# The same 2997 steps of a DeltaNet and MLP kernel, emitted in another stated order

## The chip, the cores and the metric

The kernel runs on one NeuronCore of a Trainium2 chip, in fp32. The metric is the device time of one execution in microseconds, median over the runs. Profiles come from one further execution under the hardware profiler; their "span" runs from the first to the last instruction.

## The reference, cut to what matters

Attention works on batch 4, 8 heads, 768 tokens and head dimension 48; the bridge puts the heads side by side into 384 columns, and a layernorm with an MLP 384 to 1536 to 384 follows.

```python
def _attn_ref(q, k, v, beta):
    k_n = k / (np.linalg.norm(k, axis=-1, keepdims=True) + 1e-06)
    state = np.zeros((B, H, D, D), dtype=np.float32)
    for t in range(S):
        kt, vt, bt = (k_n[:, :, t], v[:, :, t], beta[:, :, t, None])
        y[:, :, t] = np.einsum('bhd,bhde->bhe', q[:, :, t], state)
        v_old = np.einsum('bhde,bhd->bhe', state, kt)
        state = state + bt[:, :, :, None] * np.einsum('bhd,bhe->bhde', kt, vt - v_old)
    return y

def _moe_ref(x, g_ln, w_ch1, w_ch2):
    mu = np.mean(x, axis=-1, keepdims=True)
    var = np.mean((x - mu) ** 2, axis=-1, keepdims=True)
    xn = (x - mu) / np.sqrt(var + 1e-06) * g_ln
    ch = np.maximum(xn @ w_ch1, 0.0) @ w_ch2
    return x + ch
```

## The kernel before

The 768 tokens are cut into 12 chunks of 64. Inside a chunk the recurrence over tokens is turned into matrix products and the inverse of a triangular 64x64 matrix for each of the 32 batch-heads; between chunks a 48x48 state for each batch-head is carried on.

**Attention on TensorE.** All 32 batch-heads of a chunk are worked on together. One step of this kind issues 64 small matmuls, one for each of 32 heads in two passes of fp32, in tiles of 64*64 of the array, so that several heads run beside each other. `gram` and `queries` (L775) make the products k k' and q k'; `recur` makes the state's share of values and outputs (L983), the solved values u (L1017; L1000 for chunk 0), the output (L1024) and the state's update (L1034). Steps of 32*32 tiles, `join` (L898 and L904), put the halves of an inverse together.

**The inverse.** Chunk 0's is made by `first_inverse` on three engines, since all else waits for it: VectorE scales the products (L695), masks (L704) and transposes them (L710), then five rounds follow, each with two products E (L722) and two products Z (L741) on TensorE, one for each half of the heads, masked copies on VectorE (L731), transposes (L687) and copies on ScalarE (L681). The other chunks' 32x32 halves are inverted row by row on VectorE by `rows_inverse`, a multiply (L860) and a subtraction (L867) for each row, for two chunks at a time.

**MLP.** A chunk of 64 tokens of 4 batches is 256 rows. The first layer is L1326 and L1341 for chunk 0, L1300 for chunks 1 to 3, and `fifteen` (L1221), a product scheme with 15 products where the plain one has more, from chunk 4 on. The second layer is `seven` (L1423), a scheme of seven products on halves, with its sums and differences on POOL (L1410). These matmuls use the array as a whole (128*128). Ahead of them the layernorm (its reciprocal root on VectorE is L967) is made.

**Weights.** They come as 64-bit words in ten pieces (`fetch`, on ScalarE's DMA queue) and are turned into fp32 by `convert` on ScalarE (L524, L532), VectorE (L529) and POOL (L542).

**What sets the order.** The program first records steps: `add` notes a function that issues some instructions of one engine, and works out which earlier steps it depends on. `emit` then runs the steps in the sequence that the string `ORDER` states, each number one step and `a:b` a stretch; "z" is one additional full-array product whose result is used by nobody (L1515). A step may stand anywhere behind the steps that it depends on.

```python
    def emit(self):
        out = set()
        for n in stated_order():
            if n < 0:
                self.filler()
                continue
            fn, deps = self.steps[n]
            assert deps <= out and n not in out
            fn()
            out.add(n)
```

`in_this_order` ties every instruction to the one before it on its engine, and the DMA issues of SyncE and ScalarE to each other, so that the stated sequence is the sequence that runs. Only the order within each engine's own list (and of the DMA issues) has an effect on the chip.

Steps that the prediction names: 95 and 96 are the first products of chunk 0 (L635), 97 and 98 transposes for chunk 1 (L568); 110 and 116 are the scaling L695 for the two halves of the heads, 111 and 117 the masks L704, 112 and 118 the transposes L710; 122 and 124 are E1, 126 and 132 Z1, 144 and 150 Z2, 162 and 168 Z3, 180 and 186 Z4; 149 is a copy on ScalarE behind Z2, 161 a masked copy on VectorE ahead of Z3; 355 and 357 are L1000, 359 and 360 L1024 of chunk 0; 588 is the first product of the MLP (L1326). 51 loads a part of chunk 0's keys on SyncE's queue.

Of the kernel before, what the change touches and what calls it, by code (L numbers as in the profile page):

```python
# [59 lines left out]
1 9 49 50 8 63 52 51 10 5 250 54 71 11 56 0 6 14 7 12 47 62 53 48 23 13 72 55 36 18 64 42 26 37 61 27 58 60 77 81 15 28 17 32 331 43 73 88 29 40 65 79  # L60
24 19 82 68 78 21 89 74 95 16 76 20 90 75 98 83 80 84 22 85 34 91 86 96 87 33 25 92 97 93 4 35 30 94 110 99 100 111 101 112 114 66 116 122 113 211 210
117 102 70 208 123 115 103 118 233 126 104 124 69 127 105 107 128 119 31 121 106 125 120 252 129 223 132 38 221 138 108 134 39 139 109 222 251 140 135
204 131 130 234 136 3 674 144 137 67 57 133 213 254 146 224 141 149 2 209 413 235 44 142 147 45 253 244 212 143 256 145 150 255 242 205 41 154 153 416
155 243 148 238 151 236 332 152 225 675 156 z 215 157 240 159 158 214 237 239 160 216 162 161 257 46 241 168 164 166 333 206 165 334 245 207 417 163
419 169 174 170 343 258 226 175 172 259 173 415 171 176 381 177 425 260 227 261 167 178 344 217 228 180 179 248 414 263 345 335 386 346 219 182 262
677 186 264 181 420 183 265 266 192 267 268 189 246 336 269 270 218 193 229 220 188 185 184 187 59 271 196 422 190 272 191 231 273 426 194 274 197 199
275 198 421 338 276 247 355 382 277 195 249 384 356 337 359 278 678 279 679 280 200 230 281 361 232 363 387 339 282 364 201 383 391 283 202 203 385
389 373 357 284 375 388 376 374 396 285 590 390 340 358 341 588 591 286 681 342 401 379 287 392 288 289 594 394 290 953 291 347 589 595 292 348 380
293 360 393 350 598 294 362 395 592 368 599 349 442 295 680 441 406 296 351 427 369 815 593 444 297 814 428 443 298 676 602 424 299 352 687 596 300
603 353 301 445 302 399 303 304 377 597 612 305 817 306 606 354 307 418 308 613 607 309 365 423 600 310 397 311 614 689 312 601 366 313 610 314 816  # L70
315 615 611 316 409 604 317 819 318 319 616 818 605 320 404 321 617 322:324 407 608 398 483 325 378 400 402 326 367 629 487 609 370 481 403 371 618
630 480 429 372 446 627 486 485 619 682 628 405 482 633 484 631 329 634 408 330 447 632 410 327 328 448 449 956 479 821 635 820 411 637 809 620 810
638 488 636 621 489:491 641 492 494 622 639 430 493 691 623 495 640 690 496 642 431 497 686 498 624 499 500 822 643 435 434 693 645 501 433 962 502
688 432 503 644 651 957 1100 504 505 436 692 506 507 652 438 508 439 509 647 440 510 437 811 653 511 512 964 450 666 1102 513 654 514 1099 451 515 655
516 517 454 518 965 519 966 1104 520 656 961 455 521 951 456 452 522 463 958 457 646 458 657 453 1215 464 649 465 807 523 459 658 808 524 466 460 1105
525 659 963 467 461 1106 694 950 468 683 462 955 526 660 1112 527 684 1101 528 469 1111 529 473 648 650 695 530 475 474 531 470 476 532 471 661 472
696 533 857 534 1114 535 697 536 967 855 537 858 1213 538 539 685 662 540 856 541 823 542:545 825 546:548 861 663 549:551 863 552 862 553:556 667 867
557 864 968 668 665 869 824 879 868 702 880 959 664 960 859 1214 669 873 860 560 1272 559 672 1103 865 561 812 670 558 705 826 477 866 699 874 698 870
701 888 969 412 706 871 703 885 700 875 704 671 872 1216 566 881 889 625 876 877 895 563 1217 813 567 878 1222 890 564 569 915 882 570 827 562 891 568
886 898 571 565 916 707 1107 896 626 899 572 1115 1212 900 708 883 576 892 709 574 884 901 573 1224 710 1116 893 575 902 954 887 894 917 903 1380 1113  # L80
828 904 1221 1558 711 713 905 829 923 918 577 712 897 924 832 714 715 673 925 716 833 717 906 718 834 926 719 912 835 907 841 836 927 1274 842 919 928
837 1560 908 838 929 920 843 913 839 909 844 941 840 720 910 721 830 845 921 914 846 847 722 922 1377 851 723 578 1264 1223 849 930 724 1557 1226 579
942 725 580 1562 831 931 1218 852 943 850 1118 853 932 848 726 581 1117 933 854 727 582 944 911 728 934 945 729 935 730 970 936 1227 731 938 1376 583
732 937 971 1225 972 585 1273 1228 584 587 1210 1563 733 946 734 1006 952 735 939 736 737 1004 738 974 973 947 1005 739 1007 586 1028 1010 740 1029
1119 1564 1559 975 1229 1011 1031 1008 1561 741 1385 742 1570 940 743 1569 1012 744 1009 745 746 1016 747 1013 976 748 749 1014 1387 750 1017 1572
1386 751 478 1211 979 752 1571 1015 1378 753 754 977 980 755 981 756 1018 1389 757 988 982 989 1384 1573 978 990 1379 1020 983 758:760 1022 761 1021
762 991 984 763 1390 1019 764 1108 985 765 949 1023 1034 1391 766 1230 986 767 948 1109 768 769 1388 1037 770 987 771 1110 1026 772 773 992 774 775
993 994 1038 776 1027 1024 995 1670 1044 1231 996 1030 1120 1265 1025 1275 1047 1035 1121 1039 1064 1040 1048 1122 1045 780 1041 1032 777 1049 1033
778 1065 1042 1036 779 1050 1043 1066 1126 1046 1051 1000 1054 1219 1266 1233 998 1268 997 1232 1276 999 1267 1127 1052 1055 1131 1053 1067 1565 1128
1061 1056 1072 1124 1270 1068 1125 1073 1392 1220 1069 1129 1074 1002 1057 1130 1001 1070 1075 785 1003 784 1058 1269 1076 781 1234 1079 1277 782 1059  # L90
1080 1271 783 1060 1077 1081 1680 2035 1078 786 1373 1062 1090 787 1123 1082 790 1091 789 1083 788 1063 1278 1092 2037 1279 1084 1682 1132 1071 1093
1681 1085 791 1302 1133 1086 1280 793 1134 792 1135 794 1136 1138 795 1094 1284 1137 2039 1139 1140 1235 1141 1285 1142 1281 1143 796 1305 1095 1303
1236 1668 1290 2034 1096 1684 1144 1087 1374 1145 2041 1282 1146 1291 1673 2036 1147 1148 1574 1088 1149 1237 1150 1283 1669 1151 1152 1239 1098 1153
1154 797 1155 1156 1296 1157 799 800 1158 1241 1686 1159 1288 1576 1160 1297 1304 1248 1161 2040 1311 1162 1289 1286 1238 1249 1250 1163 1381 1294
1164 1858 1287 1382 1165 1240 1383 1679 801 1312 1675 1295 1292 1251 1089 1166 1167 1685 1313 1168 1293 1674 1393 1252 1242 1169 798 1253 1855 1308
1243 1395 1375 1309 1244 1857 1306 1245 802 1318 1397 1097 1314 1300 1394 1319 1307 1298 1170 1575 1301 1171 803 805 1172 1246 1321 1173 1315 1247
1174 1322 1299 1255 1316 804 1310 806 1323 1254 1317 1396 1175 1256 1320 1683 1176 2038 1398 1672 1177 1178 1324 1179 1399 1338 1180 1325 1676 1181
1339 1326 1340 1327 1328 1182 1341 1260 1346 1183 1342 1184 1257 1347 1185 1343 1186 1259 1348 1344 1329 1687 1258 1349 1335 1353 1330 1350 1187 1354
1863 1188 1331 1189 1853 1351 1190 1402 1336 1191 1263 1345 1352 1261 1400 1262 1192 1404 1193 1194 1355 1865 1411 1195 1332 1412 1196 1356 1197 1413
1364 1198 1333 1414 1365 1334 1337 1450 1199 1441 1366 1200 1401 1440 1451 1455 1201 1427 1403 2150 1577 1357 1405 1430 1406 1367 1851 1358 1457 1439  # L100
1566 1852 1415 1431 1456 1359 1416 1429 1407 1688 1443 1408 1859 1567 1432 1409 1418 1368 1444 1202 1452 1410 1435 1203 1369 1433 1204 1454 1458 1370
1205 2047 1453 1417 1208 1460 1434 1459 1419 1361 1862 1464 1442 1461 1568 1436 1462 1866 1466 1437 1671 1467 1463 1867 1438 1578 1465 1360 1445 1690
1362 1446 1469 1468 1579 1447 1689 1422 1428 1471 1448 1470 1449 1474 2049 1472 1477 1581 1584 1475 1473 1580 1480 1860 1423 1861 1478 1363 1483 1479
1481 1583 1476 1691 1421 1484 2051 1489 1420 1694 1486 1485 1582 1693 1490 1692 1487 1502 1496 1588 1491 1503 1587 1488 1677 1492 1678 1504 1695 1585
1493 1206 1505 1494 1586 1506 1497 1495 1371 1701 1426 1516 1869 1589 1498 1696 1703 1868 1507 1499 1699 1529 1207 1424 2042 1509 1697 1517 1372 1744
# [1547 lines left out]
```

## Time and profile before

| | |
|---|---|
| median of 3 runs | 507.94 us (506.93 to 510.24) |
| span of the profiled execution | 508.8 us, mean granted TensorE clock 0.965 |
| TensorE busy, by stretch: 0 to 15 / 15 to 44 / 44 to 66 us | 10.7 of 15 / 21.7 of 29 / 20.4 of 22 us |
| TensorE busy, 66 to 500 us | 431.2 of 434 us |
| TensorE's granted clock, 15 to 44 / 44 to 66 us | 0.59 / 0.77, else 1.00 until 500 us |
| VectorE, ScalarE, POOL busy from 66 to 500 us | 298, 203 and 239 of 434 us |
| start of the first MLP product (step 588) | 55.9 us |
| start of E1 (step 122) | 13.46 us |

The profiled execution has no run time of its own beside its span; the span is 0.9 us above the median of the runs and lies inside their spread. Busy time of a matmul record is from its start to a modelled end, so that consecutive records overlap; the distance from one start to the next is the better measure of what a step takes. Every fp32 matmul of the program appears as two records, a transpose as one.

### The profile page before, as it was taken

The page shows a single profiled execution, that of the slowest core. Times are in us where ns is not written, and L with a number is a line of the kernel's source. Part 1 is how long each engine was busy: PE and PEld are TensorE (multiplying, and loading weights), DVE is VectorE, ACT ScalarE, POOL GpSimd, SP SyncE. Part 2 cuts the span into 40 slices and gives each one's busy share as a digit, 9 for nine tenths or more (in the row PEclk, how much of TensorE's full clock was granted, in tenths as well). Part 3 has the DMA queues.
Part 4 walks back from the last instruction along what each step waited for, and adds up shares of the span by engine and source line. Part 5 has one row for each costly group of instructions (what it writes and reads, how often), then busy time and mean ns, then how long its engine had stood idle before and what let it go on. Part 6 is the DMA issues. An engine that isn't in the chain of part 4 may idle for free.

```text
span 508.8 us, 22190 instructions
## 1 busy us (share of the span) xinstructions
PE 488.6 (96%) x9606; PEld 447.6 (88%) x9606; DVE 353.8 (70%) x780; ACT 249.0 (49%) x620; POOL 275.6 (54%) x430
## 2 busy tenths in 40 slices
PE   7778999999899999999999999999999999999996
PEld 3667988788788898899999999999999999999996
DVE  9668987997679648896649898568899328143251
ACT  5758873643544524627435535435563257363230
POOL 5464537264755496438894363492543850645633
PEclk9756799999999999999999999999999999999999
DMA  8988796667656566546834434766154402211101
GB/s 168 293 160 190 249 200 85 98 152 130 90 86 87 187 119 119 65 99 149 194 58 62 94 62 135 150 94 97 50 92 106 111 20 45 60 48 46 24 18 31
DMA packets 196097, 54.99 MB, mean 108 GB/s; under 512 B 186076, under 2 KB 189404, under 8 KB 196000
## 3 DMA queue, kind: packets, MB, share of 16 engines
q1 hardware_dynamic: 189920, 40.58, 41.9%
q10 hardware_dynamic: 3872, 9.83, 6.0%
q0 software_dynamic: 2208, 3.17, 3.8%
q8 instruction: 75, 1.23, 1.0%
q14 instruction: 22, 0.18, 0.1%
HBM read 36.64 MB, written 16.91 MB: 105 GB/s over the span
## 4 chain that ended last, share of the span: by engine, by line
PE 90%; DVE 5%; issue 2%; POOL 1%; DMA 1%; SPq 0%; ACT 0%; DVEq 0%; POOLq 0%; ACTq 0%
PE f L1423 29%; PE f L1221 22%; PE f L1300 9%; PE f L1326 4%; PE f L1341 3%; PE by L983 2%; PE by L1024 2%; PE two L983 2%; PE by L775 2%; PE two L1017 2%; PE two L775 2%; PE two L1034 2%; PE f L775 1%; DMA xt<-xd 1%; PE by L741 1%
## 5 line engine op out<-in xcount | busy, mean ns | idle before, releaser
L1410 POOL TENSOR_TENSOR h_all<-h_all 128x256 f32<-128x256 f32 x123 | 89.9, 742 | 135.1 <-PE f L1423 121.3
L1423 PE MATMUL f<-w_sb,h_all 128*128 128x192 f32 x492 | 109.8, 332 | 1.6 <-DVE rstd L967 1.6
L1423 PEld LDWEIGHTS f<-w_sb,h_all 128*128 128x128 f32 x492 | 81.8, 190 | 3.6 <-issue 1.9
L1423 PE MATMUL f<-words,h_all 128*128 128x192 f32 x396 | 84.5, 330 | 0.3 <-POOL h_all L1410 0.3
L860 DVE TENSOR_TENSOR tmp<-xb,gb 128x87 f32<-128x87 f32 (+21 forms) x186 | 73.7, 396 | 4.9
L867 DVE TENSOR_TENSOR xb<-xb,tmp 128x87 f32<-128x87 f32 (+21 forms) x186 | 73.6, 396 | 4.8
L1241 DVE TENSOR_TENSOR h_all<-h_all,f 128x512 f32<-128x512 f32 x96 | 63.5, 682 | 14.3 <-PE f L1221 13.2
L1423 PEld LDWEIGHTS f<-words,h_all 128*128 128x128 f32 x396 | 66.6, 190 | 1.7 <-POOL h_all L1410 1.0
L1300 PE MATMUL f<-xnt,w_sb 128*128 128x256 f32 x216 | 50.2, 382 | 0.0
L349 POOL DMA_DIRECT2D tb<-in_k_dram x64 | 42.0, 660 | 10.3 <-DVE kt L755 9.4
L1243 ACT ACTIVATE h_all<-h_all 128x512 f32<-128x512 f32 x48 | 28.5, 624 | 34.6 <-DVE h_all L1241 34.3
L1300 PEld LDWEIGHTS f<-xnt,w_sb 128*128 128x128 f32 x216 | 40.2, 190 | 5.3
L1237 ACT COPY h_all<-f 128x512 f32<-128x512 f32 x48 | 26.2, 590 | 34.3 <-PE f L1221 17.4
L1441 DVE TENSOR_TENSOR o<-f,x 128x192 f32<-128x192 f32 x33 | 11.6, 352 | 38.9 <-PE f L1423 22.3
L1221 PE MATMUL f<-words,w_sb 128*128 128x128 f32 x256 | 31.7, 276 | 0.0
L1309 ACT ACTIVATE h_all<-f 128x256 f32<-128x256 f32 x36 | 13.3, 382 | 35.1 <-PE f L1300 34.9
L1221 PEld LDWEIGHTS f<-words,w_sb 128*128 128x128 f32 x256 | 30.0, 192 | 0.2
L1221 PE MATMUL f<-xnt,w_sb 128*128 128x128 f32 x192 | 25.4, 276 | 0.0
L542 POOL TENSOR_TENSOR w_sb<-words 128x768 uint32<-128x768 uint32 (+1 forms) x11 | 15.0, 1365 | 17.7 <-DVE words L529 13.3
L1221 PEld LDWEIGHTS f<-xnt,w_sb 128*128 128x128 f32 x192 | 23.7, 192 | 0.1
L1326 PEld LDWEIGHTS f<-xnt,w_sb 128*128 128x128 f32 x144 | 19.2, 200 | 3.3 <-issue 0.2
L1088 ACT ACTIVATE xnt<-xnt,g_sb 128x256 f32<-128x256 f32 x27 | 12.5, 498 | 19.2 <-DMA xnt<-xld 19.1
(246 smaller groups left out, 958.4 us busy)
## 6 DMA issues: line engine op xcount, KB each, us to landing
words<-in_moe_w_ch_dram ACTq DMA_DIRECT2D x10, 768.0 KB, 5.2
gd<-gsb SPq DMA_DIRECT2D x11, 512.0 KB, 3.6
v<-in_v_dram SPq DMA_DIRECT2D x24, 192.0 KB, 4.3
kr<-in_k_dram SPq DMA_DIRECT2D x46, 96.0 KB, 3.6
out_dram<-o SPq DMA_DIRECT2D x44, 96.0 KB, 2.8
xld<-xlt SPq DMA_DIRECT2D x9, 384.0 KB, 3.3
xnt<-xld SPq DMA_DIRECT2D x36, 96.0 KB, 3.2
gb<-gd SPq DMA_DIRECT2D x44, 64.0 KB, 3.0
```

Source lines behind the costliest of these rows:

```text
L349: add(eng, cost, lambda: QUEUE[eng].dma_start(out=out_, in_=in_), r, w, bulk=n * ns / 16e3, **kw)
L775: nc.tensor.matmul(pair[hp][half(e ^ (hp & n)), (g * NP + j) * C : (g * NP + j + 1) * C], kt[drows(hp), l], rt[drows(hp), i],)
L860: lambda j=j, n=n, w=w, t=t: nc.vector.tensor_tensor(out=t, in0=xv[:, 0:n, j : j + 1].to_broadcast([np_, n, w]), in1=gv[:, j : j + 1, j + ...
L867: "DVE", dve(n * w), lambda t=t, rest=rest: nc.vector.tensor_tensor(out=rest, in0=rest, in1=t, op=ALU.subtract),
L1221: nc.tensor.matmul(wide(p[:, 128 * n : 128 * n + 128]), w[n // 2][:, n % 2 * 128 : n % 2 * 128 + 128], r, start=start and n == 0, stop=Tru ...
L1237: add("ACT", act(512), lambda: nc.scalar.copy(o, p), pk, ok)
L1241: add("DVE", dve(512), lambda: nc.vector.tensor_tensor(out=o, in0=o, in1=p, op=op), pk, ok)
L1243: add("ACT", act(512), lambda: nc.scalar.activation(o, o, ACTF.Relu), [], ok)
L1300: nc.tensor.matmul(p[:, 0:TOK], w1_sb[:, t, f * 128 : (f + 1) * 128], xnt[:, t], start=(t == 0), stop=(t == KC - 1))
L1326: nc.tensor.matmul(p[:, 0:128], w1_sb[:, t, f * 128 : (f + 1) * 128], xnt[:, t, cols], start=(t == 0), stop=(t == KC - 1))
L1410: add(eng, cost, lambda: e.tensor_tensor(out=out_, in0=x, in1=y, op=op), r, w, port=2 if eng == "Pool" else 1, pr=-2)
L1423: lambda f=f, t=start and f == 0: nc.tensor.matmul(p[:, 0:D2], lhs(f), rhs[:, f], start=t, stop=(f == F2 - 1), skip_group_check=True),
```

## The change

The string `ORDER` is replaced. No step is added, taken away or altered, and the rest of the file is the same to the letter; the string is 11 lines shorter, so that a line L in the profile before is L - 11 behind the change. Both strings hold the numbers 0 to 2996 once each and one "z". The longest sequence that the two have in common is 911 steps; half of the steps move by ten places or fewer, few by more than a hundred. Steps are moved on all engines, the DMA issues among them. The beginning of both, and the stretch of the new order around step 588:

```diff
 ORDER = """
-1 9 49 50 8 63 52 51 10 5 250 54 71 11 56 0 6 14 7 12 47 62 53 48 23 13 72 55 36 18 64 42 26 37 61 27 58 60 77 81 15 28 17 32 331 43 73 88 29 40 65 79
-24 19 82 68 78 21 89 74 95 16 76 20 90 75 98 83 80 84 22 85 34 91 86 96 87 33 25 92 97 93 4 35 30 94 110 99 100 111 101 112 114 66 116 122 113 211 210
-117 102 70 208 123 115 103 118 233 126 104 124 69 127 105 107 128 119 31 121 106 125 120 252 129 223 132 38 221 138 108 134 39 139 109 222 251 140 135
-204 131 130 234 136 3 674 144 137 67 57 133 213 254 146 224 141 149 2 209 413 235 44 142 147 45 253 244 212 143 256 145 150 255 242 205 41 154 153 416
-155 243 148 238 151 236 332 152 225 675 156 z 215 157 240 159 158 214 237 239 160 216 162 161 257 46 241 168 164 166 333 206 165 334 245 207 417 163
...
+49 8:12 38 47 62 5 71:73 50 52 36 63 56 51 0 20 17 1 37 6 7 74 40 251 77 78 48 32 58 42 44 81 88 13 82 89 26 76 14 80 83 68 84 2 21 79 85 86 55 416 65
+54 53 675 60 64 61 98 33 70 90 91 27 92 210 96 97 95 100 99 101 102 24 93 18 19 15 75 87 110 28 16 111 34 35 115 114 103 104 94 116 23 22 117 112 122
+118 123 67 4 121 233 69 223 113 124 125 66 120 119 126:128 30 244 221 242 222 243 132 137 129 235 107 131 138 139 133 29 134 250 245 135 211 130 136
+217 109 106 219 209 108 238 234 140 144 147 146 145 45 677 57 39 46 41 236 25 218 31 220 414 105 256 253 255 333 254 334 331 424 413 425 344 426 332
+423 422 418 z 141 142 204 156 143 157 158 150 152 151 225 148 227 224 212 252 213 215 149 155 154 162 205 257 258 239 259 153 159 260 226 160 261 3
...
+385 360 590 588 379 340 341 396 394 362 591 288 388 289 390 365 392 401 589 380 290:300 393 395 681 347 594 592 441 348 442 593 595 349 444 443 598
+599 350 596 445 351 342 419 815 817 597 368 397 406 600 602 352 353 601 604 603 366 605 354 814 301:324 369 398 325 446 612:615 608 606 616 617 399
...
 """
```

TensorE's steps around step 588, taken from the two strings, are

```
before: ... 355 359 200 339 373 357 590 588 379 594 347 348 360 598 592 442 441 351 602 596 445 377 612 ...
after:  ... 355 336 359 200 339 357 373 360 590 588 379 347 594 592 441 348 442 598 596 445 351 600 602 ...
```

In the order before, TensorE's attention steps from step 588 on stand in 69 uninterrupted groups among the full-array steps: 43 of one step (28 products, 15 joins), 23 of two and 3 of three. In the new order they stand in 87 groups: 78 of one step (59 products, 19 joins), 8 of two and 1 of three.

163 rows, old and new, of the table ORDER are left out of this document.

## The prediction

> **What bounds the kernel now.** I read the page first, then the chain of work that ended last for 5 to 60 us, then TensorE's instructions in order of time in three stretches, then VectorE's in the first 15 us. The page (busy time, clock by slice, DMA queues, shares of the chain):
>
> ```profile
> PE 488.6 (96%) x9606; PEld 447.6 (88%) x9606; DVE 353.8 (70%) x780; ACT 249.0 (49%) x620; POOL 275.6 (54%) x430
> ...
> PEclk9756799999999999999999999999999999999999
> ...
> q8 instruction: 75, 1.23, 1.0%
> ...
> PE 90%; DVE 5%; issue 2%; POOL 1%; DMA 1%; SPq 0%; ACT 0%; DVEq 0%; POOLq 0%; ACTq 0%
> ```
>
> TensorE is busy for 96% of the 508.8 us and is 90% of the chain; no other engine is above 70%. An order can therefore gain only where TensorE idles, and can lose wherever it makes TensorE's own work longer. The granted clock is low in slices 2 to 5 alone. The idle time sits at the front. The busy time by stretch is 32.4 us of the first 44 and 20.4 us from 44 to 66. From 66 to 500 us I find only four gaps in TensorE: 0.19 us at 131, 1.76 at 139.9, 0.81 at 143.8 and 0.44 at 496. All that is to be gained behind 66 us is about 3.2 us.
>
> Some of the early idle time has no engine behind it. From the chain of 5 to 60 us (start, duration, what):
>
> ```profile
> 15.53 1.12 PE f L741 x30
> 16.65 1.10 issue
> ...
> 22.60 0.37 PE f L775 x21
> 22.97 1.60 issue
> ...
> 28.02 0.63 PE f L775 x21
> 28.64 0.85 issue
> ...
> 34.05 0.62 PE by L741 x18
> 34.67 1.53 issue
> ```
>
> Each gap breaks off in the middle of a step of 32 matmuls, where nothing is waited for. Between one gap and the next lie 128 matmuls, that is 256 instructions with their weight loads. The instruction queue moved 1.23 MB in 75 packets, 16.4 KB each; at 16 DMA engines x 508.8 us x 1.0% / 75 one takes 1.09 us. So TensorE's program comes in blocks of 256 instructions, and these four blocks came late: 5.08 us. Counting the compiled instructions of each order (four for a matmul of fp32, two for a transpose, one for a semaphore), all four gaps and the fifth at 143.8 lie at places 193 or 194 modulo 256.
>
> **The cost of leaving the full array.** TensorE's instructions in order of time, 293 to 300 us (start, duration of the group; steps of two records):
>
> ```profile
> 294.46 0.49 PE L1423 MATMUL f<-words,h_all 128*128 128x192 f32 x2
> ...
> 295.44 0.49 PE L1423 MATMUL f<-w_sb,h_all 128*128 128x192 f32 x2
> 295.76 0.49 PE L1423 MATMUL f<-words,h_all 128*128 128x192 f32 x2
> 296.18 1.15 PE L1017 MATMUL two<-v,xt 64*64 64x48 f32 x64
> 297.26 0.59 PE L1423 MATMUL f<-words,h_all 128*128 128x192 f32 x2
> 297.69 0.49 PE L1423 MATMUL f<-w_sb,h_all 128*128 128x192 f32 x2
> ```
>
> L1423 steps follow each other every 0.325 us. The last one ahead of the attention group L1017 (64*64 tiles) takes 0.42 (295.76 to 296.18), L1017 takes 1.08, and the first L1423 behind it 0.43. Where a second attention group follows, the first takes 0.97. So one group alone between full-array steps pays 0.093 + 0.110 + 0.104 = 0.307 us; of two together the second still takes 1.04, so they pay 0.093 + 0.075 + 0.104 = 0.272; a lone join (L898, L904, 32*32 tiles: 0.683 in every place) pays 0.197. These are the same to 0.01 us in all 71 L1423 steps next to a group.
>
> **The change part by part.** No step is added, removed or altered; 2997 steps keep their work, and each engine runs its own in the new order.
>
> (1) Attention groups among the MLP's matmuls. From the first L1326 step (588) on, the order before leaves the full array 69 times: 28 lone product groups, 15 lone joins, 23 pairs, 3 triples. The new one leaves it 87 times: 59, 19, 8 and 1. Before: 28 x 0.307 + 15 x 0.197 + 26 x 0.272 = 18.6 us. After: 59 x 0.307 + 19 x 0.197 + 9 x 0.272 = 24.3. With TensorE saturated this lies wholly on the path: +5.7 us. Low bound: 18 more departures at a lone join's 0.197, +3.5. High bound: 18 pairs split at 2 x 0.307 - 0.272, +6.2. The Trainium skill, TensorEngine Tiling (Array Packing), section Key Properties, states that changing the tiling mode drains TensorE. The rows agree as far as each crossing costs about 0.1 us; by that rule alone, 36 more crossings of 0.1, an estimate, the sum would be 2.1 us less.
>
> (2) Chunk 0's inverse, ahead of the MLP. It is a chain of TensorE, VectorE and ScalarE, so what is put in front of one link is paid. VectorE now has 5.11 us of work from step 110 (L695 at 11.14) through what E1 (step 122, L722) waits for and its mask copy 123, against 3.46: the second head group's scaling and mask come ahead of the first's transpose. That is +1.65. Ahead of the mask copy 161 (L731 at 33.42), which Z3 waits for, VectorE has 2.2 us more (sums and converts). SyncE issues a key load (51) third instead of second: +0.9, about one issue slot. ScalarE has 6.5 us more ahead of copy 149 (L681 at 25.62), nine weight converts, against 2.7 us of its idle time there (0.46, 0.56, 1.71 of its gaps): up to +3.8, of which I take half, since the totals ahead of the last inverse steps differ by only 0.8 us. Sum 1.65 + 2.2 + 0.9 + 1.9 = 6.65.
>
> Against it stands the block fetch. The boundaries now fall into steps 124, 144, 150, 168 and 186, and TensorE waits longer for VectorE ahead of 144 and 168, so the next block has time to land; I keep one such gap of 1.6 of the four, -3.5. The new order also runs step 360 (L1024, 0.97 us) ahead of 588, in time in which before waits there (0.7 us for DVE u L1005): -1. Net 6.65 - 3.5 - 1 = +2. Bounds: 1.65 - 3.5 = -2 where only the first item counts, and +6.5 where no fetch gap goes. The Trainium skill, Runtime: NRT & Kernel Launch, section Instruction fetch mechanics, says that crossing a block boundary is mostly hidden. The four gaps above, 5.08 us, say otherwise for this stage; behind 150 us no gap here contradicts it. By the rule throughout, nothing would be returned by the fetch and this part would be +5.6, an estimate.
>
> (3) Block boundaries behind the first MLP step. The trace's 75 packets stand one to one against the 75 boundaries. A packet starts 1.2 us (median) after the boundary is some 32 instructions ahead, takes 1.1 and is usable 1.4 later: 3.7. In that count the shortest block before has 3.7 us, the shortest of the new order 4.0. Neither stalls; the gap at 143.8 followed a wait. 0.
>
> (4) Waits behind 55 us. Before has 3.2 us from 66 on and 1.7 between 55 and 64. The wait at 139.9 is for DVE rstd L967, queued behind row operations L860/L867 that started when DMA xt<-xd landed at 135.69; SyncE's queue ahead of it, its loads and stores, is rearranged, as are POOL's h_all L1410. The DMA engines have room there (share 0.71 from 66 to 130 us, 0.44 from 146 to 500), so a moved transfer is late by its place in SyncE's queue, some 0.6 us for each issue put ahead of it. New waits may come in the first MLP chunk, where L1326 follows its ReLU with fewer attention groups between. Between -5 and +3; I take -1, the wait at 139.9 shortened by half.
>
> Sum against the profiled execution: span 508.8 + 5.7 + 2 + 0 - 1 = **515.5 us**. The median of the runs is 507.94, 0.9 below that span, so **514.6** in the metric.
>
> **Rivals.** (a) The early chain loses in full: +6.5 in part 2 instead of +2, and no wait is returned: 508.8 + 5.7 + 6.5 = 521, in the metric 520. For it: DVE 9.0 busy of the first 10 us. Against it: the totals ahead of the inverse's end are nearly equal.
>
> (b) Faster: the early block gaps decide. If all four go (-5.1), VectorE's added work lies beneath other waits, and VectorE's operations that POOL now holds up in the first 10 us go free (L402 took 2.38 us at 3.80 and 1.06 at 6.09, beside 0.18 to 0.19 at other times: -3), and the waits of part 4 vanish (-4.9), it is 508.8 - 5.1 - 3 - 4.9 + 5.7 = 501.5, metric 500.6. It decides from where step 588 starts before 48 us (55.87 now). Against it: E1 is gated by the longer VectorE queue.
>
> ```profile
> 3.58 0.19 DVE L402 TENSOR_SCALAR xb<-xb 128x64 int32<-128x64 int32 x1
> ...
> 3.80 2.38 DVE L402 TENSOR_SCALAR xb<-xb 128x64 int32<-128x64 int32 x1
> 6.09 1.06 DVE L402 TENSOR_SCALAR xb<-u 128x64 int32<-128x64 int32 x1
> ```
>
> (c) No difference: the early part returns about as much as the departures cost (part 2 at -2, part 4 at -3): 508.8 + 5.7 - 5 = 509.5, metric 508.6.
>
> **How the numbers follow.** Forecast 0.52, (a) 0.15, (b) 0.08, (c) 0.25. A measurement here tells about 1% from no change, 502.9 to 513.0. Faster is (b): 0.08. Same is (c) and a sliver of the forecast's own spread: 0.27. Slower: 0.65. The range reaches from 505.5, part 2 and 4 near their low bounds, to 523, where (a) meets 2 us of new waits: 508.8 + 5.7 + 6.5 + 2.
>
> **What would show it.** TensorE's busy time about 6 us longer with the same 9606 matmuls; L1423's mean above 332 and 330 ns; E1 starting at 15 to 16 us instead of 13.46; step 588 at 56 to 61 us; fewer "issue" gaps ahead of 40 us, and none behind 150. Wrong: TensorE's busy time within 2 us of 488.6 (departures cost nothing more), or step 588 ahead of 52 us.

## The result, and the profile after

The changed order takes **527.09 us** (median of 4 runs, 525.65 to 529.22) against 507.84 for the order before on the same chip (506.93 to 510.24): 1.037 times as long, 95% interval 1.034 to 1.041. The prediction said slower, 514.6 us and at most 523.

The profiled execution of after has a span of 523.5 us and a time of its own of 525.65, the shortest of the four. In the kernels below, too, the time is the span and 1.7 to 2.2 us. The span of 508.8 before thus belongs to one of the longest runs before, and the two traces differ by 14.7 us where the medians differ by 19.25.

The page of after (busy time, shares of the chain):

```profile
PE 498.0 (95%) x9606; PEld 451.7 (86%) x9606; DVE 356.7 (68%) x780; ACT 249.6 (48%) x620; POOL 277.9 (53%) x430
...
PE 87%; DVE 4%; ACT 3%; DMA 2%; POOL 2%; issue 1%; ACTq 0%; DVEq 0%; POOLq 0%
```

The matmuls are the same 9606, and TensorE is busy for 9.4 us longer. In the chain "issue" falls from 2% to 1%, but ScalarE rises from nothing to 3%, DMA from 1 to 2% and POOL from 1 to 2%.

Step 588, of the first MLP products (590, a product of the same kind, runs just ahead of it in both orders), starts at 63.52 us instead of 55.87: 7.65 us are lost ahead of it. It is a noisy mark: over the profiles below it lies between 54.1 and 55.9 us where the early steps are all in the order before (before, early_before, before_split, before_cm2700), and between 63.5 and 67.8 where they are all in the new order (after, early_after, after_merge, after_cm2700). From it to the start of the last matmul it is 455.7 us instead of 448.2: 7.5 us more. The stretch from E1 (step 122) to step 588, as columns of length, busy time of TensorE, weight loads, VectorE, ScalarE and POOL, granted clock, DMA share and GB/s; of before, then of after:

```profile
13.46:55.87 42.41, 33.17 (x923) 29.14 (x924) 31.58 (x82) 30.48 (x76) 22.24 (x28) 0.60 0.88 212
```

```profile
16.24:63.52 47.28, 35.36 (x924) 30.92 (x924) 31.81 (x87) 28.93 (x74) 23.58 (x28) 0.54 0.75 182
```

E1 starts 2.8 us later. Behind it TensorE idles for 11.9 us instead of 9.2, and the same number of matmuls takes it 2.2 us longer, at a granted clock of 0.54 instead of 0.60. Where the stretch is lost shows in the chain of work that ended last (start, duration, what):

```profile
14.49 6.76 DMA tb<-in_q_dram
...
24.79 0.37 ACT xt L670
...
26.04 0.56 ACT h_all L513
...
27.10 0.54 ACT h_all L521
...
28.21 0.78 ACT words L513
28.99 0.16 ACT xt L670
```

Two places stand out. A tile of q (`tb`) is issued only at 14.49 and ends the wait at 21.3. And between two copies of the inverse (`xt`, L670) ScalarE runs three weight converts (L513, L521; 1.9 us on the chain) and two q copies (26.61 and 27.73): step 144, ahead of them, starts at 24.45 (24.81 before), step 150 behind them at 33.41 (26.88). Step 150 before, then after (TensorE in order of time):

```profile
26.88 1.14 PE L741 MATMUL by<-xt,gsb 64*64 64x64 f32 x32 [0.60 <-DVE gsb L731]
```

```profile
33.41 1.11 PE L730 MATMUL by<-xt,gsb 64*64 64x64 f32 x32
```

The lines that answer to the attention group among the MLP's steps, and the one larger gap behind 150 us that nothing explains (TensorE in order of time, 229 to 234 us):

```profile
229.62 1.15 PE L972 MATMUL by<-s_all,qt 48*64 48x48 f32 x64
230.69 0.59 PE L1412 MATMUL f<-w_sb,h_all 128*128 128x192 f32 x2
232.01 1.27 PE L1006 MATMUL two<-v,xt 64*64 64x48 f32 x64 [0.73 <-issue]
233.21 0.59 PE L1412 MATMUL f<-words,h_all 128*128 128x192 f32 x2
```

The lone group at 229.62 takes 1.07 us from start to start, as before; the one behind the gap takes 1.20. Of the early fetch gaps one is left, 0.74 us at 53.17, where before had 5.08 us in four.

### The profile page after: what moved, and what is told of

The parts are those of the page before. It is cut to its first block, busy times and chain, and to the rows that moved or that the text cites. A ratio compares the mean times of both kernels' runs of the same rounds, so it can differ in the third digit from the quotient of the medians.

```text
span 523.5 us, 22161 instructions
## 1 busy us (share of the span) xinstructions
PE 498.0 (95%) x9606; PEld 451.7 (86%) x9606; DVE 356.7 (68%) x780; ACT 249.6 (48%) x620; POOL 277.9 (53%) x430
## 4 chain that ended last, share of the span: by engine, by line
PE 87%; DVE 4%; ACT 3%; DMA 2%; POOL 2%; issue 1%; ACTq 0%; DVEq 0%; POOLq 0%
PE f L1412 28%; PE f L1210 20%; PE f L1289 9%; PE f L1315 4%; PE f L1330 3%; PE by L1013 2%; PE two L972 2%; PE two L1006 2%; PE by L972 2%; PE two L764 2%; PE two L1023 2%; PE by L764 2%; DMA tb<-in_q_dram 1%; DVE xb L856 1%; DMA words<-in_moe_w_ch_dram 1%
## 5 line engine op out<-in xcount | busy, mean ns | idle before, releaser
L1412 PE MATMUL f<-w_sb,h_all 128*128 128x192 f32 x492 | 100.0, 332 | 0.0
L1412 PEld LDWEIGHTS f<-w_sb,h_all 128*128 128x128 f32 x492 | 80.1, 190 | 2.2 <-DVE o L1430 0.3
L856 DVE TENSOR_TENSOR xb<-xb,tmp 128x87 f32<-128x87 f32 (+21 forms) x186 | 78.2, 420 | 4.8
L1230 DVE TENSOR_TENSOR h_all<-h_all,f 128x512 f32<-128x512 f32 x96 | 63.5, 681 | 21.1 <-PE f L1210 18.3
L1412 PE MATMUL f<-words,h_all 128*128 128x192 f32 x396 | 77.2, 330 | 0.0
L1412 PEld LDWEIGHTS f<-words,h_all 128*128 128x128 f32 x396 | 65.2, 190 | 1.1 <-POOL h_all L1399 0.3
L1289 PEld LDWEIGHTS f<-xnt,w_sb 128*128 128x128 f32 x216 | 39.8, 190 | 5.6
L1210 PE MATMUL f<-words,w_sb 128*128 128x128 f32 x256 | 32.9, 278 | 1.1 <-DVE o L1430 1.1
L1008 ACT COPY u<-two 128x768 f32<-128x768 f32 x11 | 8.8, 799 | 35.5 <-PE two L1006 35.5
L1210 PEld LDWEIGHTS f<-xnt,w_sb 128*128 128x128 f32 x192 | 23.7, 191 | 0.4
L1051 ACT ACTIVATE x<-by 128x384 f32<-128x384 f32 x23 | 11.2, 487 | 24.9 <-PE by L1013 15.5
```

The lines of the kernel that those rows point to most:

```text
L856: "DVE", dve(n * w), lambda t=t, rest=rest: nc.vector.tensor_tensor(out=rest, in0=rest, in1=t, op=ALU.subtract),
L1210: nc.tensor.matmul(wide(p[:, 128 * n : 128 * n + 128]), w[n // 2][:, n % 2 * 128 : n % 2 * 128 + 128], r, start=start and n == 0, stop=Tru ...
L1230: add("DVE", dve(512), lambda: nc.vector.tensor_tensor(out=o, in0=o, in1=p, op=op), pk, ok)
L1289: nc.tensor.matmul(p[:, 0:TOK], w1_sb[:, t, f * 128 : (f + 1) * 128], xnt[:, t], start=(t == 0), stop=(t == KC - 1))
L1412: lambda f=f, t=start and f == 0: nc.tensor.matmul(p[:, 0:D2], lhs(f), rhs[:, f], start=t, stop=(f == F2 - 1), skip_group_check=True),
```

## The experiments

All are orders of the same steps; "before" and "after" below are the two orders. Each was timed in three rounds or more beside before, whose median lay between 507.8 and 509.3; amounts are the ratio less 1, times 508.4. Their order strings have as many lines as that of before, so lines of the profiles below carry the numbers of before; where after itself is quoted, they are 11 lower.

**Which half of the order?** The two orders are cut behind step 588.

```diff
 early_before: the steps through 588 as before, the rest as changed
 early_after:  the steps through 588 as changed, the rest as before
```

> The order before up to step 588, the changed order for all later steps. Theory: the loss has two parts that add, one ahead of step 588 (7.6 us between the two traces) and one behind it (7.3 us: 5.2 for 18 more departures from the full array, 2 for waits). Then step 588 starts at 56 us again and the time is 508 + 7 = 515 us. Rival: the later loss is a consequence of the late start (loads, inverses and weights that come late keep TensorE waiting); then it is within 2 us of before, 508 to 510.

> The changed order up to step 588, the order before for all later steps. Theory: step 588 starts at 63 to 64 us, TensorE is saturated behind it in either order, and the time is 508 + 7 = 515 us; early_before and this one together give the whole loss of 19 us only if the parts add, 14 to 15 by the traces. Rival: behind 588 the order before has waits of its own (4.5 us) that a later start hides, then 510 to 512.

early_before took 517.56 us (1.0185, 1.0158 to 1.0211), early_after 518.67 (1.0182, 1.0112 to 1.0252). The late half loses 9.4 us and the early half 9.3, the latter within wide bounds (5.7 to 12.8); together that is the whole loss. The late half reads out of the trace: from step 588 to the last matmul 457.1 us against 448.2, +8.9. By the start-to-start times of the prediction (1.08 for a lone group, 0.325 and the crossings for L1423, and so on) its steps add up to 449.4 against 443.5, which is +5.9; what is left, called waits here, is 7.7 against 4.7, +3.0. This split is made with the price table itself. Without the table, TensorE's busy time from step 588 on is 452.7 us against 445.8, +6.9, and its idle time rises by 1.9.

**The price of a departure.** Among before's steps behind 588, 26 pairs of small groups are taken apart by a full-array step, so that it leaves the full array 95 times instead of 69.

```diff
-... 447 448 635 637 ...
+... 447 635 448 637 ...
 (26 such places)
```

> The order before, with 26 pairs of neighbouring attention steps behind step 588 taken apart by exchanging the second with the full-array step behind it; nothing else moves, and departures from the full array rise from 69 to 95. Theory: each split costs 0.34 us for two products (0.20 or so with a join), 8.4 us by the rows, all on the path: 516 us. Rival: the start-to-start differences are an artefact of the records or lie beside waits, then 508 to 510.

514.89 us (1.0128, 1.0104 to 1.0152): +6.5. TensorE in order of time, 291 to 294 us:

```profile
292.04 0.59 PE L1423 MATMUL f<-w_sb,h_all 128*128 128x192 f32 x2
292.56 1.15 PE L983 MATMUL two<-s_all,kt 48*64 48x48 f32 x64
```

The step between two groups takes 0.52 us, which is the 0.325 and the two crossings of 0.093 and 0.104. By the table the steps add up to 451.9 us, +8.4; that is the price and not a measurement. Measured is the stretch from step 588 to the end, of before, then of before_split (length, then TensorE's busy time first):

```profile
55.87:508.80 452.93, 445.81 (x8558) 413.30 (x8557) 310.04 (x658) 211.04 (x529) 246.80 (x386) 1.00 0.48 97
```

```profile
54.09:513.00 458.91, 453.66 (x8558) 414.95 (x8557) 309.07 (x658) 210.98 (x529) 245.37 (x386) 1.00 0.47 95
```

With the same 8558 records of matmuls TensorE is busy for 7.9 us longer, a little under the price. The stretch grows by only 6.0, because idle time falls by 1.9: the wait at 139.9 us went. The departures are a cost that lies on the path.

**Would fewer departures help?** Small groups are brought together: in after_merge 35 pairs (departures 87 to 56, 8.6 us less by the table), in after_cm2700 25 pairs chosen so that no instruction block gets short (-7.4), in before_cm2700 11 pairs (-3.2).

```diff
-... 448 635 620 621 431 ...
+... 448 431 635 620 621 ...
 (35, 25 and 11 such places)
```

> The changed order with 35 pairs of attention groups behind step 588 brought together, the full-array steps between them (2.7 us or less) put ahead or behind; nothing else moves. Departures fall from 87 to 56. By the departures' price alone 8.6 us less, 518.5 us. Theory with the block fetch: two or more groups of 64x64 tiles together run through 256 instructions in 1.9 to 2.3 us, shorter than the 3.5 to 4.0 us that a fetch takes, so ten or so gaps that nothing explains in mid-run appear, 10 to 14.6 us by the count of boundaries: 528 to 533 us. That is, the lone groups are what keeps the blocks long.

> The changed order with 25 pairs brought together, only those by which no block of 256 instructions becomes shorter than the fetch. Departures price: 7.4 us less; no new gaps by the count of boundaries. Both theories 519 to 521 us; if waits for other engines take the place of the departures, 523 to 526.

> The order before with 11 pairs brought together in the same way, with the blocks respected; departures fall from 69 by 11 or so. By the rows 3.2 us less than before, 505 us, as long as no wait takes their place; the rival is that waits do (the split of 26 pairs returned 2.5 us of waits, so a merge may bring some): 507 to 509.

568.43 us (1.1154), 543.59 (1.0676) and 519.67 (1.0226): each far slower than it started, and no theory had that. In after_merge what the steps behind 588 take beyond the table rose to 58.6 us. Some 35 us of it are idle time of TensorE. Its busy time there rose as well, to 463.4 us against 452.2 in after, although the table has it fall by 8.6: the mean granted clock of the stretch is 0.97 instead of 1.00. Waits of TensorE by line (total, times, longest):

```profile
PE by L1024 <- ACT u L1019: 5.6, 6, 0.9
PE f L904 <- ACT es L910: 3.3, 2, 1.7
```

A group that uses what ScalarE copies out of the group ahead of it (L1019 out of L1017, L910 out of L898) waits 0.9 to 1.7 us for the copy when the two stand side by side, as in each of these eight waits. The MLP steps between them had covered that. before_cm2700 has the same L910 wait, 3.3 us. So a lone group costs 0.307 us and can save up to 1.7; a price of departures alone leaves that out. With one more such wait on L904 for L910 (1.6), the pairs of this kind make 10.5 of the 35 us; the others are waits for other results of ScalarE and VectorE, each of 2.3 us or less. Gaps that nothing explains make 4.1 us, against the 10 to 14.6 that short blocks were to make, so these are not the main cause.

**Early: ScalarE and the loads, or VectorE?** before_act_early is before with ScalarE's instructions and all loads up to 588 in the changed order; before_dma with the loads alone; before_actc with ScalarE's compute alone. before_dve has VectorE's first 48 steps as changed; after_dvepool_before is the changed order with VectorE and POOL up to 588 as before.

```diff
 before_act_early = before_dma and before_actc together
 before_dma, order of loads:
-49 50 52 51 54 56 53 55 64 61 60 331 65 68 66 70 69 ...
+49 50 52 56 51 68 55 416 65 54 53 60 64 61 70 67 69 66 ...
 before_actc, ScalarE:
-... 104 119 121 120 129 223 221 108 109 135 131 130 136 ...
+... 223 113 120 119 244 221 242 137 129 235 131 135 211 130 136 217 109 219 209 108 ...
 before_dve, VectorE (and the reverse in after_dvepool_before):
-1 10 5 11 0 14 12 47 23 13 18 26 27 15 ...
+10 11 12 47 5 0 20 17 1 13 82 89 26 76 14 ...
```

> The order before, but ahead of step 588 ScalarE's instructions and the DMA issues of SyncE and ScalarE stand as in the changed order; TensorE, VectorE and POOL as before. Theory: copy 149 behind Z2 waits again behind nine weight converts (it started 3.3 us later in the changed trace) and the q tile for steps 107 and 106 lands late, so step 588 comes 4 to 6 us later: 512 to 514 us. Rival: VectorE's order makes the early loss, then 507 to 510.

> The order before with the DMA issues of SyncE and ScalarE ahead of step 588 in the changed order's sequence, the five first weight pieces behind the same ScalarE steps as there; all compute instructions of all engines as before. Theory D: the whole early loss, step 588 at 62 to 66 us, 515 to 519 us. Theory A: 508 to 511 us.

> The order before with ScalarE's compute instructions ahead of step 588 in the changed order's sequence, nine more weight converts ahead of copy 149 among them; DMA issues in the sequence before. Theory D: 508 to 511 us, the converts find time where TensorE's program is late. Theory A: 514 to 519 us. With before_act_early (both together, 518.6) the two parts show whether they add.

> The order before, with only VectorE's first 48 steps in the changed order (the second head group's scaling and mask ahead of the first's transpose, the step behind 123 included); all other engines and the loads as before. The prediction priced this at +1.65 us at E1 (step 122) and let it pass down the chain. Theory A (ScalarE's order and the loads alone make the early loss): E1 moves from 13.46 to 15-16 us, and the later waits of the chain swallow most of it; step 588 at 55.5-56.5, time within 1.0 us of before. Theory B (the chain passes each microsecond on): step 588 at 57.5-59, time 1.7 to 2.8 us above before.

> The changed order, with VectorE's and POOL's steps up to 588 in the order of before; ScalarE's, SyncE's and TensorE's as changed. Theory A (ScalarE and the loads make the early loss): the time stays within 2 us of the changed kernel's 527.1, E1 still waits for the late q tile or starts earlier with the time lost again behind it. Theory B (VectorE's queue carries the 2.8 us by which E1 starts later, and more behind it): 521 to 524.5 us, step 588 at 61-64.

| kernel | median, us | ratio (95%) | E1 / step 588 at |
|---|---|---|---|
| before_act_early | 518.61 | 1.0212 (1.0152 to 1.0273) | 13.8 / 62.5 |
| before_dma | 512.87 | 1.0077 (1.0047 to 1.0107) | 13.6 / 58.3 |
| before_actc | 521.14 | 1.0242 (1.0179 to 1.0304) | 13.5 / 65.3 |
| before_dve | 508.75 | 1.0022 (0.9997 to 1.0047) | 16.9 / 56.2 |
| after_dvepool_before | 526.67 | 1.0349 (1.0315 to 1.0384) | 14.6 / 63.4 |

before_act_early and before_actc cost more than any theory had allowed, and before_dma lies between its two; the two of VectorE went as theory A said. VectorE's order makes little or nothing of the loss. In before_dve E1 starts 3.4 us late, and step 588 only 0.3. With VectorE and POOL put back, the changed order starts E1 1.6 us earlier and step 588 at the same place. ScalarE and the loads alone are enough for the whole early loss (10.8, with an interval of 7.7 to 13.9, beside 9.3). The loads alone make 3.9, ScalarE's compute alone 12.3 (9.1 to 15.5), so the parts do not add. In before_actc, TensorE's longest wait and a ScalarE step (in order of time):

```profile
PE f L775 <- ACT qt L573: 6.9, 1, 6.9
```

```profile
52.40 0.21 ACT L935 ACTIVATE knrm<-ksum 128x16 f32<-128x16 f32 x1 [2.06 <-DMA ksum<-gd]
```

L775 waits for a q copy that ScalarE runs only at 29.07, behind converts and copies of the inverse; ahead of these ScalarE had stood 1.75 us for a weight piece (L532 at 20.09) and 2.42 us for a transpose of VectorE (L681 at 24.67). And `knrm` (step 427) holds ScalarE's queue for a load that the order of loads before issues late.

**Which ScalarE steps?** before_conv puts eight weight converts earlier, before_qt two q copies (108, 109) later, before_conv_qt both, before_427 step 427 alone, some 40 places earlier.

```diff
 before_conv:
-... 104 119 121 120 129 223 221 108 109 135 ... 213 149 209 235 147 244 242 ...
+... 104 119 244 121 120 129 235 223 221 242 108 109 135 ... 213 215 149 209 238 147 225 ...
 before_qt:
-... 221 108 109 135 131 130 136 137 213 149 ...
+... 221 135 131 130 136 137 213 109 108 149 ...
 before_427:
-... 219 183 189 246 ...
+... 219 183 427 189 246 ...
```

> The order before with eight of the nine weight converts on ScalarE (215, 219, 225, 227, 235, 238, 242, 244) put where the changed order has them among its neighbours, ahead of copies of the inverse; the copies qt L573 (109, 108) stay where they were, and nothing else moves. If the converts make the loss (each takes 0.55 to 0.95 us and stands still where its weight piece has not landed), most of the 12 us of before_actc: 515 to 521 us. If the late copies of q do, 508 to 511 us.

> The order before with the two copies qt L573 (109, 108) on ScalarE seven and eight places later, behind the copies of Z1 and convert 213, as in the changed order; converts as before. Step 204 on TensorE (L775) needs them and stands ahead of Z2's and E3's steps; it waited 6.9 us for them in before_actc. If their place makes the loss: 512 to 518 us. If the converts do: 507 to 511 us.

> The order before with both moves of before_conv and before_qt: eight converts ahead and the two copies of q (109, 108) behind them. If the loss is their product (the copies of q stand behind converts that wait for weights, and step 204 on TensorE behind these copies), more than the 3.7 us of the parts together: 514 to 520 us. If they only add, 511 to 513 us, and the rest of before_actc's 12 us is elsewhere on ScalarE.

> The order before with one step of ScalarE moved: 427, the root of chunk 1's key norms (knrm L935, started at 62.3 us), stands behind 183, among the copies of Z4 as in the changed order, forty places earlier. It waits for two loads ksum of SyncE, of which the second is issued at 43.7 us in the order before and lands 5 us later. In before_actc it started at 52.4 us and held three copies of the inverse up. If this is the rest of the loss: 512 to 516 us. If not: 507 to 510 us.

The converts cost 3.7 us, well under the expected 7 to 13 (511.93; 1.0073, 1.0049 to 1.0097), the q copies nothing (508.60; 0.9999, 0.9975 to 1.0022), both together 4.8 (513.25; 1.0094, 1.0069 to 1.0120), not told apart from the converts alone. Step 427 alone costs 7.3 (515.03; 1.0144, 1.0108 to 1.0180). ScalarE of before_427, in order of time:

```profile
48.41 0.22 ACT L935 ACTIVATE knrm<-ksum 128x16 f32<-128x16 f32 x1 [7.47 <-DMA ksum<-gd]
48.53 0.25 ACT L681 COPY xt<-by 128x128 f32<-128x128 f32 x1
```

A step of 0.22 us, moved, stalls the queue for 7.47, and the inverse's copy L681 stands behind it; TensorE's L741 waits 7.1 for that. 4.8 and 7.3 come near the 12.3 of before_actc, but in before_actc `knrm` ran 4 us later and stood only 2.06 us, so that the same two causes make its 12.3 is not shown.

**The loads of before in the changed order.** If the loads' order cost 3.9 us, putting it back in the changed kernel should return some of it.

```diff
 after_dma, order of loads:
-49 50 52 56 51 68 55 416 65 54 53 60 64 61 70 67 69 66 ...
+49 50 52 51 54 56 53 55 64 61 60 331 65 68 66 70 69 ...
```

> The changed order with the DMA issues of SyncE and ScalarE ahead of step 588 in the sequence before; all compute instructions as changed. Theory D: early loss of 10 us returned, 517 to 520 us, as early_before. Theory A: 525 to 528 us.

535.55 us (1.0533, 1.0488 to 1.0578), 8.2 slower than the changed kernel; both theories missed. ScalarE of after_dma:

```profile
59.38 0.21 ACT L935 ACTIVATE knrm<-ksum 128x16 f32<-128x16 f32 x1 [11.39 <-DMA ksum<-gd]
```

In the changed kernel the same step ran at 46.34 without a wait, since its loads had gone out earlier too. So step 427 is no cost of the change itself: the new order of loads feeds the new order of ScalarE, and neither can be priced by itself.

**Why does the q tile come late?** SyncE's queue in after and in after_68 (start, duration):

```profile
7.31 0.67 SPq L338 DMA_DIRECT2D v<-in_v_dram  x1
14.49 0.59 SPq L338 DMA_DIRECT2D tb<-in_q_dram  x1
```

```profile
8.03 1.06 SPq L349 DMA_DIRECT2D tb<-in_q_dram  x1
```

SyncE stands still for 6.5 us. The semaphores that the trace notes for each load tell why: the loads of SyncE and ScalarE signal through eight semaphores in rotation, and a load waits for the one that the load eight places ahead of it signals. In the changed order the q tile (step 61, place 13 counted from 0) stands eight behind a 768 KB weight piece (step 68, place 5); the piece lands at 14.47 us, and the q tile is issued at 14.49. before issues that piece at place 13. SyncE's waits for weight pieces in after (total, times, longest):

```profile
SPq L338 <- DMA words<-in_moe_w_ch_dram: 12.7, 3, 6.5
```

Two orders test it: step 61 moved ahead of 68 (after_q), and 68 moved behind 61 (after_68).

```diff
-       49 50 52 56 51 68 55 416 65 54 53 60 64 61 70 67 ...
+after_q:  49 50 52 56 51 61 68 55 416 65 54 53 60 64 70 67 ...
+after_68: 49 50 52 56 51 55 416 65 54 53 60 64 61 68 70 67 ...
```

> The changed order with one step moved: 61, the load of the second half of chunk 0's q tile, stands ahead of 68, the issue of the first weight piece, instead of seven places behind it. In the changed order 61 is the 14th issue of SyncE's and ScalarE's queues and in the compiled program waits for the completion semaphore of the 6th, the 768 KB weight piece that landed at 14.47 us; it was issued at 14.49 instead of 8. Theory: this late tile delays the transposes 107 and 106, all of TensorE behind them and copy qt L573; step 588 comes 3 to 6 us earlier and the time falls from 527 to 521 to 524 us. Rival: ScalarE's weight converts ahead of copy 149 set the early part, and the tile lands beside them: 526 to 528 us.

> The changed order with one step moved: 68, the issue of the first 768 KB weight piece, stands behind 61 instead of ahead of 55, so that it is the 14th issue and not the 6th, as in the order before. In the compiled programs every issue of SyncE and ScalarE waits for the completion of the one eight places ahead. after_q moved that wait from 61 to the second weight piece on ScalarE, where it stood from 9.8 to 15.3 us and held the norms up, so its time said nothing of the tile. Theory D (the wait for a weight piece eight issues ahead makes the early loss): the q tile is issued at 8 us, step 588 starts at 56 to 60 us, 518 to 522 us. Theory A (ScalarE's converts ahead of copy 149 make it): 525 to 528 us.

after_q took 528.99 us (1.0395, 1.0352 to 1.0438): no gain. The load that now stands eight behind 68 is step 70, on ScalarE. It is issued only at 15.35, and ScalarE's next step waits behind it:

```profile
15.74 0.21 ACT L596 ACTIVATE knrm<-ksum 128x8 f32<-128x8 f32 x1 [4.67 <-DMA words<-in_moe_w_ch_dram]
```

after_68 took 523.85 (1.0308, 1.0257 to 1.0358), 3.2 us below the changed kernel and between its two theories. The intervals of the two overlap, so the gain rests on the trace as well: step 588 starts at 61.39 us, below the 63.5 to 67.8 of the four profiles with the whole early part changed. It is still slower than before; no order tried beats before.

## Why the prediction was right or wrong

**Part 1, departures: right.** +5.7 predicted. With the changed late half TensorE is busy 6.9 us longer behind 588 (6.4 in after itself), and in before_split 7.9 where the table gave 8.4. Two crossings of 0.1 us alone, the other price weighed there, would have made 3.6 and 5.2; the runs go with the rows. The indicator for it was chosen badly: L1412's mean stays at 332 and 330 ns, because a record does not hold the crossing ahead of it; only distances between starts do. TensorE's busy total rose by 9.4, not 6: 6.4 behind step 588 and 3.1 ahead of it, 2.2 of these behind E1, where the granted clock was 0.54 instead of 0.60. A lone join does not take 0.683 in every place, as I wrote: 11 of the 15 do, the others 0.71 us or more.

**Part 2, the early chain: wrong, and this made the miss.** +2 predicted (-2 to +6.5); +9.3 measured by early_after (5.7 to 12.8), +7.65 between the two traces. Two steps failed: the 4.5 us of returns, which did not come, and the price of ScalarE's and SyncE's queues. That the terms to be paid, 6.65, come near the loss is luck: 3.85 of them were VectorE's, which cost next to nothing. Term by term:

- VectorE, +1.65 and +2.2: nothing that can be told from noise (before_dve +1.1 with an interval that holds zero, after_dvepool_before the same as the changed kernel). E1 was late as I said, 16.24, but that delay is taken up by the waits behind it.
- SyncE, +0.9 for one place in the queue: the loads alone cost 3.9, and undoing one step of them returned about 3.2. I counted places, about one issue slot each; what counts is which load stands eight places ahead.
- ScalarE, +1.9: the mis-sized term. In the order before, the eight converts alone cost 3.7, ScalarE's whole order alone 12.3, with the new loads 10.8. I halved the 3.8 "since the totals ahead of the last inverse steps differ by only 0.8 us". That is where the argument failed. A queue that runs in order is held by the first step whose input has not come (weights, a sum, a q tile), and the amount of work ahead of a step says nothing of that. Of the changed kernel's 9.3, about 3.2 are shown by moving step 68. For the converts 3.7 to 4.8 are taken over from the order before; no run put them back in the changed order, and after_dma warns against such a transfer. The last 1.3 to 2.4 us are not settled.
- The returns, -3.5 and -1: the fetch gaps did go (5.08 to 0.74), but TensorE waited for data in their place: from E1 to step 588 it idles 11.9 us instead of 9.2. So their going returned nothing that can be seen. That TensorE would have waited in that time anyway is the likely reason, but it is argued and not shown. Rival (a), the early chain losing in full with no wait returned, was the right case; its 6.5 lies inside the interval, but it left out the waits of part 4.

**Part 3, instruction blocks: nearly right.** No stall of weight; one gap of 0.73 us ahead of step 1398, in after and in early_before at the same step, and in after one of 0.28 in the middle of a step (L1006 at 140.9), against "none". Whether a block or something else makes them was not tried.

**Part 4, waits behind 588: wrong.** -1 predicted (-5 to +3), +3.0 by the table in early_before, at the upper bound; +1.9 where idle time alone is counted. The wait at 139.9 went altogether, where I had taken half, but new ones came that I had not looked for. The largest of TensorE's waits behind step 588 by line, after (the last holds the two gaps of part 3):

```profile
PE by L1085 <- ACT xnt L1100: 1.3, 1, 1.3
PE f L1210 <- DVE o L1430: 1.1, 1, 1.1
PE two L1006 <- issue: 1.0, 2, 0.7
```

The sum that the runs give is 5.9 + 9.3 + 3.0 = 18.2 of the 19.25 us between the medians, with the early part uncertain by 3.5 either way.

## What to carry to other kernels

Price a moved step by when its inputs land, not by how much work stands ahead of it: on an in-order engine a 0.2 us step put ahead of its load held everything behind it for 7 to 11 us. Look in the compiled program at which load's completion each load waits for, since one big transfer moved forward delays the small one a fixed number of places later, on whichever engine that falls. Filler between dependent small steps costs a crossing but hides the copy between them, and two reorderings that fit each other cannot be priced, or undone, one at a time.

## What the runs showed of the hardware

Short waits in the middle of a run were followed by a lower clock, though not each time. TensorE of after_merge around 146 us in order of time, and its windows (length, busy time of the engines, granted clock, DMA share, GB/s):

```profile
145.70 0.74 PE L904 MATMUL f<-xt,es 32*32 32x32 f32 x64 [1.68 <-ACT es L910]
146.37 4.67 PE L1423 MATMUL f<-words,h_all 128*128 128x192 f32 x16
```

```profile
143.00:147.00 4.00, 2.32 (x135) 1.97 (x134) 0.00 (x0) 2.66 (x8) 3.92 (x6) 1.00 0.85 113
147.00:151.00 4.00, 4.00 (x15) 3.63 (x14) 1.33 (x3) 1.16 (x4) 3.99 (x7) 0.57 0.74 69
```

After a wait of 1.68 us the granted clock falls to 0.57 for 4 us, and eight L1423 steps take 4.5 us, 0.56 each instead of 0.325: 1.9 us more on top of the wait itself. It came again with a wait of 1.63 us at 161 (0.51 from 161 to 168), but not with one of 1.63 us at 462 in the same run, nor with the 1.76 us at 139.9 in before, where the windows show 1.00 on both sides; what decides is not settled here. The Trainium skill, TensorE: Matmul & The Clock Gate, section on HAM oscillation, sets the bound at idle gaps of about 3.4 us; here the lower clock came twice beside waits of less than half of that.

A load waiting for the completion of the load eight places ahead of it, across two engines' queues, was not expected either: 6.5 us of a still SyncE in after, 4.67 us on ScalarE in after_q.
